# First batch's attention denominators from key sums of their own, an earlier load of the first weights, and a later preparation of the second batch, in a cosformer attention + mixture-of-experts kernel

## Chip, cores, metric

One core of a Trainium2 chip. The metric is the device time of one execution in microseconds (us), lower is better. A clock is the share of TensorE's full speed that was granted, 1.00 or, as half clock, 0.50. The profile's span is one execution's, and is some 1.7 us shorter than the time measured for the same run.

## The reference, cut to what matters

```python
def phi(x, c, s):                        # q, k, v: (8 batches, 8 heads, 576, 64)
    r = np.maximum(x, 0.0)
    return np.concatenate([r * c, r * s], axis=-1)
q_p = phi(q, cos_w, sin_w)
k_p = phi(k, cos_w, sin_w)
kv = np.einsum('bhsf,bhsd->bhfd', k_p, v)
z = np.sum(k_p, axis=2)
num = np.einsum('bhsf,bhfd->bhsd', q_p, kv)
den = np.einsum('bhsf,bhf->bhs', q_p, z)[..., None] + 1e-06
x = num / den                            # then as (4608, 512)
# gates exp(x @ w_gate), 8 rounds of row and column balancing; then for 8 experts
#   out += P[:, e] * (relu(x @ w1[e]) @ w2[e])
```

## The kernel before

The first 60 us prepare the attention of the eight batches one after the other and begin the first expert's two layers as soon as a batch is there. The work is written in "slots": after each piece of the first expert (first-layer tile `ft4` to `ft7`, then halves of second-layer tiles) the functions hung on that slot are issued. Program order is kept on each engine (in the trace before, VectorE's `q_p` at 34.35 us stood behind a `zsel` that had waited 2.84 us), so the slot decides who stands behind whom. A "turn" transposes a third of one head pair's q on TensorE, and an "eviction" copies a result out of TensorE's output memory.

```python
te, ve, se = ...            # TensorE, VectorE, ScalarE, each kept in written order

def prep_k(b, hk):          # relu of k: ScalarE for b >= 1, VectorE for b == 0
def prep_kp(b, hk):         # k_p = relu(k) * (cos | sin), VectorE
def prep_v(b, hk, copy):    # copies v beside a column of ones, into v_aug
def prep_q(b, hk):          # q_p = q * (cos | sin), VectorE; three q_p buffers;
                            #   for b >= 2 a DMA transposes it into q_pT, on SyncE's queue
def turn(b, hk, i):         # b < 2: three matmuls with the identity turn a third of q_p,
                            #   ScalarE or VectorE evicts it with a relu
def sums_begun(b, half):    # k_p^T [v | 1]: numerator matrix, and z from the column of ones
def sums_made(b, half, ps): # kv_sb (ScalarE) and zsel = z spread over a mask (VectorE)
def denominators(b):        # 24 matmuls zsel x q_pT, then epsilon, reciprocal,
                            #   and hi, hl: the reciprocal made ready for TensorE in f16
def attend(b, hk):          # needs hl and kv_sb: divides, writes xT

# first batch
for hk in range(HK):
    prep_q(0, hk)
    for i in range(3):
        turn(0, hk, i, True)
for hk in range(HK):
    prep_k(0, hk)
    prep_kp(0, hk)
keep_busy(16)               # idle 128x128 matmuls
for half in range(2):
    prep_v(0, 2 * half, se.copy)
    prep_v(0, 2 * half + 1, (se.copy, ve.tensor_copy)[half])
    begun.append(sums_begun(0, half))
    keep_busy((4, 6)[half])
... sums_made(0, 0..1), epsilons(0), denominators(0), keep_busy(34)
for hk in range(HK):
    attend(0, hk)
    prep_k(1, hk)           # the second batch's k, under the first batch's attention
    prep_kp(1, hk)
    if hk >= 2:
        prep_v(1, hk - 2, se.copy)
    ...                     # ft0 to ft3 as xT fills
prep_v(1, 2, se.copy)
prep_v(1, 3, ve.tensor_copy)
# second batch, by slot: prep_q(1, 0) and sums at 4; sums and prep_q(1, 1) at 5;
# turns of head pair hk at 5 + hk, with prep_q(1, hk + 2); denominators at 8; attend at 11 to 14
# third batch: k, q, v from slot 11 on; transposes by DMA.  Fourth batch's loads follow.
```

The softmax here doesn't subtract the row's maximum and nothing guards it: scores larger than these inputs give would overflow.

## Time and profile before

| | kernel before |
|---|---|
| time, median of its runs | 986.6 us (985.36 to 986.98) |
| TensorE busy | 969.9 of 984.8 us, mean clock 0.997 |
| first batch's attention starts | 23.16 us (its first weight load, from which the prediction counts, 23.11) |
| `ft4` starts | 30.55 us |
| second batch's attention starts | 43.69 us |
| third batch's denominators start | 57.25 us |

A window is a stretch of 3.41 us at clock 0.50, of which this trace has two (15.70 to 22.52 us). The landmarks come from the timeline of TensorE: the start in us, the length, then what ran. A batch's attention starts with its first matmul on `hl,acc_hi`, its denominators are the matmuls on `zsel`.

```profile
43.69 0.41 PE L109 MATMUL small_ps<-hl,acc_hi 96*128 96x192 f16 x3
...
57.25 0.75 PE L109 MATMUL small_ps<-q_pT,zsel 128*32 128x192 f16 x18
58.52 0.35 PE L109 MATMUL small_ps<-q_pT,zsel 128*32 128x192 f16 x6 [0.52 <-DMA q_pT<-q_p]
```

The bracket is idle time of the engine just before, and what ended it: the last six waited 0.52 us for a transposed q.

### The profile page before, as it was taken

To read this page: it belongs to the slowest core of one execution; us is meant where nothing else is said; L and a number is where in the kernel's file an instruction comes from. 1 tells how busy PE (TensorE), PEld (TensorE's weight loads), DVE (VectorE), ACT (ScalarE), POOL (GpSimd) and SP (SyncE) were. 2 spreads that over 40 slices of the span, in tenths; PEclk is the share of its full clock that TensorE was granted. 3 is DMA by queue.
4 is the path that set the end of the run, shared out by engine and by line. 5 is a ranking of instruction groups with operands and counts; after the bars stand their busy time and mean duration, and the time that the engine had idled before them with its cause. 6 is when DMAs were issued, how large, how long until landed. Compare 5 with 4: busy or idle time off the path is not lost.

```text
span 984.8 us, 20226 instructions
## 1 busy us (share of the span) xinstructions
PE 969.9 (98%) x7844; PEld 678.4 (69%) x7844; DVE 805.8 (82%) x1830; ACT 568.6 (58%) x1269; POOL 60.6 (6%) x82
## 2 busy tenths in 40 slices
PE   8999999989999999999999999999999999999997
PEld 7545444447777777777777777777777777777775
DVE  5786774789889888988789888988888888988887
ACT  5776665467776555555555555555555555555551
POOL 6311110010000000000000000000000000000001
PEclk8999999999999999999999999999999999999999
DMA  9989990741013410133103400233103401104435
GB/s 162 206 122 162 157 151 9 136 77 47 34 41 68 85 32 25 49 68 68 49 25 69 91 25 25 56 62 67 49 25 68 92 25 27 47 26 117 128 87 129
DMA packets 80336, 73.54 MB, mean 75 GB/s; under 512 B 33264, under 2 KB 72176, under 8 KB 80240
## 3 DMA queue, kind: packets, MB, share of 16 engines
q0 software_dynamic: 27232, 30.94, 20.0%
q1 hardware_dynamic: 52768, 41.06, 17.2%
q8 instruction: 61, 1.00, 0.4%
q14 instruction: 35, 0.29, 0.1%
q10 hardware_dynamic: 240, 0.26, 0.1%
HBM read 83.12 MB, written 12.98 MB: 98 GB/s over the span
## 4 chain that ended last, share of the span: by engine, by line
PE 94%; DVE 2%; DMA 2%; ACT 1%; POOL 1%; issue 0%; POOLq 0%; ACTq 0%; SPq 0%
PE rows_ps L109 34%; PE h_ps L109 28%; PE copied_ps L109 11%; PE p_ps L109 11%; PE y_ps L109 6%; PE small_ps L109 4%; DMA v_ld<-in_v_dram 1%; DMA q_pT<-q_p 0%; DVE acc_hi L847 0%; POOL hs_last L862 0%; DVE P_tok L109 0%; DMA out_dram<-acc_lo 0%; DVE colp L109 0%; ACT u L109 0%; POOL k_ld L201 0%
## 5 line engine op out<-in xcount | busy, mean ns | idle before, releaser
L847 DVE SCALAR_TENSOR_TENSOR acc_lo<-rows_ps,P_tok,acc_lo 128x512 f32<-128x512 f32 (+1 forms) x322 | 203.1, 639 | 74.8 <-PE rows_ps L109 74.7
L109 PEld LDWEIGHTS <-H 128*128 128x128 f16 x2080 | 203.0, 98 | 83.1 <-issue 1.2
L783 ACT CAST u<-h_ps 128x384 f16<-128x384 f32 x288 | 137.6, 478 | 130.7 <-PE h_ps L109 130.7
L109 PEld LDWEIGHTS <-w1e 128*128 128x128 f16 x1632 | 156.4, 98 | 66.2 <-issue 6.0
L777 DVE CUSTOM_DVE_ANT_0 H<-p_ps,u 128x384 f16<-128x384 f32 x329 | 180.9, 550 | 6.7 <-PE p_ps L109 6.6
L109 PEld LDWEIGHTS <-hs 128*128 128x128 f16 x1500 | 146.6, 98 | 56.2
L109 PE MATMUL h_ps<-S,w1e 128*128 128x384 f16 x672 | 164.1, 326 | 1.1 <-ACT u L109 0.9
L109 PE MATMUL p_ps<-xT,T 128*128 128x384 f16 x672 | 164.1, 326 | 0.1
L109 PE MATMUL rows_ps<-V,H 128*128 128x256 f16 x1000 | 150.0, 273 | 0.7 <-DVE acc_hi L847 0.7
L109 PE MATMUL h_ps<-xT,w1e 128*128 128x384 f16 (+1 forms) x616 | 150.1, 350 | 0.2 <-DVE xT L109 0.2
L109 PE MATMUL rows_ps<-w2e,hs 128*128 128x256 f16 x1000 | 150.0, 273 | 0.0
L815 ACT ACTIVATE H<-h_ps 128x384 f16<-128x384 f32 x144 | 70.6, 490 | 95.1 <-PE h_ps L109 95.1
L109 PEld LDWEIGHTS <-T 128*128 128x128 f16 x1008 | 98.1, 98 | 29.5 <-issue 3.1
L109 PE MATMUL rows_ps<-w2e,H 128*128 128x256 f16 (+1 forms) x568 | 91.2, 285 | 0.0
L796 ACT COPY copied_ps<-h_ps 128x384 f32<-128x384 f32 x144 | 67.5, 469 | 36.0 <-PE h_ps L109 35.2
L806 ACT ACTIVATE H<-copied_ps 128x384 f16<-128x384 f32 x144 | 70.8, 492 | 20.4 <-PE copied_ps L109 20.4
L109 PE MATMUL h_ps<-S,T 128*128 128x384 f16 x336 | 81.8, 325 | 0.4 <-ACT copied_ps L109 0.3
L109 PE MATMUL copied_ps<-xT,w1e 128*128 128x384 f16 x336 | 82.1, 326 | 0.0
L109 PE MATMUL copied_ps<-w2e,H 128*128 128x256 f16 x504 | 75.5, 272 | 0.0
L109 PE MATMUL rows_ps<-V,hs 128*128 128x256 f16 x500 | 74.9, 272 | 0.0
L847 DVE SCALAR_TENSOR_TENSOR acc_lo<-copied_ps,P_tok,acc_lo 128x256 f32<-128x256 f32 x126 | 60.0, 476 | 0.4
L847 DVE SCALAR_TENSOR_TENSOR acc_hi<-rows_ps,P_tok,acc_hi 128x512 f32<-128x512 f32 (+1 forms) x56 | 41.3, 737 | 20.6 <-PE rows_ps L109 19.7
(140 smaller groups left out, 956.9 us busy)
## 6 DMA issues: line engine op xcount, KB each, us to landing
S<-x_saved SPq DMA_DIRECT2D x108, 192.0 KB, 2.4
out_dram<-acc_lo SPq DMA_DIRECT2D x62, 128.0 KB, 2.4
w1e<-in_moe_w_dram POOLq DMA_DIRECT2D x7, 1024.0 KB, 9.0
w2e<-in_moe_w_dram POOLq DMA_DIRECT2D x7, 1024.0 KB, 9.6
q_ld<-in_q_dram POOLq DMA_DIRECT2D x16, 288.0 KB, 7.4
k_ld<-in_k_dram POOLq DMA_DIRECT2D x16, 288.0 KB, 8.3
v_ld<-in_v_dram POOLq DMA_DIRECT2D x16, 288.0 KB, 9.4
x_saved<-S SPq DMA_DIRECT2D x18, 192.0 KB, 1.9
```

The lines of the kernel that those rows point to most:

```text
L109: i = getattr(self.engine, name)(*args, **kwargs)
L777: latest = ve._custom_dve(TENSOR_ADD_SAT, out=out, in0=ps[:, 0:TU], in1=t[:], s0=FP32_MAX, s1=0.0)
L783: se.copy(out=t[:], in_=ps[:, 0:TU])
L796: se.copy(out=Y[:, 0:TU], in_=X[:, 0:TU])
L806: se.activation(out=h11, in_=Y[:, 0:TU], func=AF.Relu)
L815: se.activation(out=h12, in_=X[:, 0:TU], func=AF.Relu)
L847: ve.scalar_tensor_tensor(out=a, in0=rows, scalar=P_tok[:, g, self.e : self.e + 1], in1=a, op0=ALU.mult, op1=ALU.add,)
```

## The change

The first attention waited for v. The change takes the denominators' z from k and the cos/sin columns alone (`key_sums`: 72 matmuls of two columns), so that the reciprocal chain can run before v is there; the first batch's v then needs no column of ones and no copy. The start is reordered around that with fewer idle matmuls, all four parts of the first w1 load ahead of the second batch's k and v, and the second and third batches' preparation moves to later slots. The core of the diff:

```diff
-        load_w1(w0, 0, 4, (0, 1))
+        load_w1(w0, 0, 4)
         load(1, 0, "kv")
         load(1, 1, "kv")
-        load_w1(w0, 0, 4, (2, 3))
...
+        cs_half: cos columns, split by head half        # 1 memset, 2 copies, VectorE
...
-            if b:                                       # prep_k: relu on ScalarE
+            if b >= 2:
...
+        def key_sums(half):
+            for i in range(2):
+                for c in range(C):
+                    for a in range(2):
+                        te.matmul(out=z_ps[a * D : (a + 1) * D, 2 * i : 2 * i + 2],
+                                  lhsT=loaded["k", 0, 2 * half + i][:, c],
+                                  rhs=cs_half[:, c, a, :], ...)
+        def key_sums_made(half, z_ps):                  # one zsel instruction per half
...
-        (first batch as shown above)
+        for half in range(2):
+            for hk in (2 * half, 2 * half + 1):
+                prep_k(0, hk)
+            z_ps = key_sums(half)
+            keep_busy(5); epsilons and k_p 0, 1 (half 0), or k_p 2 (half 1)
+            key_sums_made(half, z_ps)
+            if half == 0:
+                denominators(0, range(0, 4))
+                keep_busy(10)
+        prep_kp(0, 3)
+        denominators(0, range(4, 8))
+        for half in range(2):
+            sums_made(0, half, sums_begun(0, half))
+            keep_busy((3, 16)[half])
         for hk in range(HK):
             attend(0, hk)
-            prep_k(1, hk)
-            prep_kp(1, hk)
-            if hk >= 2:
-                prep_v(1, hk - 2, se.copy)
-        prep_v(1, 2, se.copy)
-        prep_v(1, 3, ve.tensor_copy)
+        keys((0, 1))                    # prep_k, prep_kp, prep_v of the second batch
...
-                (second batch's slots as shown above)
+                at(0, 5, lambda: begun.append(sums_begun(1, 0)))
+                at(0, 5, keys, (2, 3))
+                at(0, 6, lambda: sums_made(1, 0, begun[0]))
+                at(0, 7, lambda: begun.append(sums_begun(1, 1)))
                 for hk in range(HK):
+                    at(0, 7, prep_q, 1, hk)
                     for i in range(3):
+                        at(0, 7, turn, 1, hk, i)
                     if hk == 0:
+                        at(0, 7, lambda: sums_made(1, 1, begun[1]))
+                at(0, 9, denominators, 1)
...
-                    (11, prep_k, 0), (11, prep_q, 0), (12, prep_k, 1), (12, prep_kp, 0), ...
+                    (12, prep_q, 0), (12, prep_k, 0), (13, prep_q, 1), (13, prep_k, 1),
+                    (14, prep_kp, 0), (14, prep_v, 0, se.copy), (15, prep_kp, 1),
+                    (15, prep_v, 1, se.copy), (15, prep_k, 2), (15, prep_k, 3),
```

## The prediction

> **What bounds the kernel now.** I read the page first: busy tenths, then the chain that ended last.

> ```profile
> PE   8999999989999999999999999999999999999997
> PE 94%; DVE 2%; DMA 2%; ACT 1%; POOL 1%; issue 0%; POOLq 0%; ACTq 0%; SPq 0%
> ```

> TensorE is the bound: 969.9 of 984.8 us busy, 94% of the chain. The change touches only the first two batches' preparation and a few slots for the third, all before 60 us. In the table by stretches TensorE is busy 10.00 of every 10 us from 60 to 190 us, and later code is unchanged. So **the whole effect is how much earlier or later TensorE reaches the third batch's denominators (58.5 us)**. TensorE idles under 15 us in all, so 2% (19.7 us) is out of reach.

> Then the chain in order of time for the start, and the stretches cut at the edges of the low clock:

> ```profile
> 5.31 8.55 DMA v_ld<-in_v_dram
> 13.88 1.25 ACT acc_lo L109 x2
> ...
> 16.10 1.16 PE small_ps L109 x36
> 17.26 0.75 PE y_ps L109 x6
> 18.01 2.19 PE small_ps L109 x28
> 20.20 3.12 PE y_ps L109 x34
> ```

> ```profile
> 12.29:15.70 3.41, 1.16 (x43) 0.91 (x41) 2.38 (x5) 2.02 (x5) 1.54 (x3) 1.00 1.34 199
> 15.70:19.11 3.41, 3.41 (x61) 2.32 (x62) 0.73 (x5) 1.15 (x5) 2.08 (x3) 0.50 1.27 205
> 19.11:22.52 3.41, 3.41 (x44) 3.09 (x39) 2.08 (x3) 0.00 (x0) 1.43 (x2) 0.50 1.23 204
> 8.00:11.41 3.41, 2.94 (x33) 1.99 (x31) 2.68 (x5) 3.38 (x10) 2.41 (x4) 1.00 1.16 185
> ```

> The chain waits for v (landed 13.86), copies it, makes k'v sums, denominators, and 34 idle matmuls (y_ps x34)[...]. Columns of the second fence after the stretch are PE, PEld, DVE, ACT, POOL busy, clock, DMA share, GB/s.[...]

> **What the change leaves waiting** shows in the timeline of the second batch:

> ```profile
> 31.82 0.69 ACT L109 COPY acc_lo<-v_ld 128x576 f16<-128x576 f16 x1
> ...
> 33.75 0.43 ACT L109 CAST kv_sb<-small_ps 128x128 f16<-128x128 f32 x2
> ...
> 34.04 0.39 DVE L109 TENSOR_TENSOR zsel<-acc_hi,small_ps 128x64 f16<-128x64 f16 x2 [2.84 <-ACT kv_sb L109]
> 34.35 0.75 DVE L109 TENSOR_TENSOR q_p<-q_ld,acc_hi 128x1152 f16<-128x1152 f16 x1
> 35.02 0.55 DVE L109 TENSOR_SCALAR q_pT<-small_ps 128x384 f16<-128x384 f32 x1
> ```

> VectorE's zsel waits behind ScalarE's kv_sb, which stands behind v copies and relus. VectorE then alternates q_p and evictions of turned q until 40.38; TensorE fills that with ft6, ft7 and four second-layer matmuls. The second batch's first attention matmul is at 43.69, the common point I compare at.

> [...]two stretches of 3.41 us at 0.50, after one 34% busy; one that is 86% busy by the records kept 1.00.[...] 16 gate matmuls of 8 columns took 0.38 us in the chain, 24 ns each.[...] The zsel above held the already loadable q_p for 2.84 us[...]. So the compiled order, which I compared between the kernels, decides.

> **The change part by part.**

> (a) *First denominators without v.* Added: 2 x 36 two-column matmuls (36 x 24 ns = 0.9 us each, an estimate from the gates). Removed: the v copies (3 ACT, 1 DVE). The added cosine copies make VectorE wait for the second sine (done 4.29), so its set-up ends near 6.6 instead of 5.0 and the first q_p near 7.4; TensorE is in its 80 idle matmuls until 7.6, so this is hidden. Then: turns of q end near 11.5; key sums to 12.5, 5 idle matmuls and the epsilons to 13.2; zsel 12.85; half the denominators (24 took 0.77 us at full clock, so 0.4) to 13.65; ten idle matmuls to 14.2. The second k lands 13.03, two relus 0.6 -> 13.66; key sums 14.2 to 15.1; zsel 15.5; denominators to 16.0; k_p to 16.2; reciprocal 1.35, hi 0.31, hl 0.41 -> **18.3**, against 22.39 before. TensorE meanwhile does both k'v sums (0.74 each) and 16 + 3 idle matmuls (56 ns) to 18.5. So attention starts near **18.5 instead of 23.11: 4.6 us gained**, if the clock stays full.

> (b) *Attention of the first batch.* The second batch's k leaves it. Then TensorE limits it: 4 x 0.85 + 16 x 0.22 plus one start-up wait = 7.1 us against 7.4. ft4 starts at 18.5 + 7.1 = 25.6, before 30.5: **4.9 ahead**.

> (c) *w1 first.* Landings are 1.3 to 1.5 us apart at about 205 GB/s. Before, w1 parts 3 and 4 landed at 25.6 and 26.9; moved ahead they land near 19.7 and 21.0, so ft4 does not wait. k and v of the second batch come 2.7 us later (k 22.4 and 25.2, v 23.8 and 26.7); w2 is still complete near 34.6.

> (d) *Second batch.* ScalarE in compiled order from 25.1: four relus (2.06) to 27.2; two v copies (1.3) to 28.5; two relus (1.1); two v copies (1.3) to 30.9; relu ft6 0.6; kv_sb at 31.5. TensorE waits near 1.2 us for the v copies before its sums. zsel ends near 32.0 to 32.4 (34.43 before): the lead is **down to 2.2**. Now q_p of head pair 0 comes after zsel (before: done at 30.46 to 31.2), and each further q_p comes after the evictions of the pair before, all in slot 7. From zsel: q_p 0.67, turns and kv_sb and second zsel 2.4 (as in the trace) -> 35.1; then three q_p (2.0), five VectorE evictions (2.5) and four hand-overs (1.3) -> 41.0, TensorE's last turn near 40.1. Unlike before, nothing fills TensorE from 31.5 to 40.1 but 36 turns (36 x 56 ns = 2.0 us). Then 8 second-layer matmuls 1.75, denominators 0.7 -> 42.6; den, reciprocal, hi, hl 2.55 -> attention at **45.2, against 43.69: 1.5 lost**.

> (e) *Third batch.* Two k_p now stand ahead of the last two q_p, so the last transposed q can come 0.67 us later; before, TensorE already waited 0.5 us there. Since 2.2 us of the chain there is transfer during other loads, I count 0 to 0.7, middle 0.4.

> Sum: 986.4 + 1.5 + 0.4 = 988.3 at full clock.

> **Rivals.**
> 1. *The clock drops in the turn phase.* 2.0 us of matmul in 8.6 is 23%, under the 34% that halved it before; 3.4 us or more of dense matmul would then run at half speed, costing 1.7 (one window) to 3.4 us (two): 990 to 992. Against it: in 8 to 11.4 us, 33 turns of 56 ns, 54% by streaming, kept full clock, so I do not know where the limit is. The key sums could halve it earlier too[...]: attention would start near 20.5. Half likely.
> 2. *Hand-overs are shorter than I count, and part of the 4.9 us lead stays.* For it: the idle matmul counts (16 ends at 18.5, hl at 18.3) look fitted to a running kernel, and so do the moved slots; one who did that saw the second batch too. Without the losses of (d) it would be 981.5; half of them gives 984 to 985. Against it: the compiled order puts zsel ahead of q_p[...].
> 3. *Transfers set the end of this phase.* If w2 (34.6) were the limit, the gain of (a) would be hidden and the time stay at 986.4. Against it: both kernels start the second layer after it has landed.

> **Range and chances.** Weights: full clock as worked out, 988.3, 0.3; clock lowered, 991, 0.3; part of the lead kept, 984.5, 0.4. The mean is 987.6; I take 987.8, as the order is compiled fact. The range, 983.5 to 992.0, holds rival 2 at its middle and rival 1 up to two half-speed windows. Faster by over 2% would need more than all idle time: 0.01. Slower by over 2% is five times the worst sum: 0.02. Within 2%: 0.97.

> **What would show each step.** (a) hl near 18.3 and attention at 18.5, clock 1.00 from 12 to 20 us. (b) ft4 near 25.6. (c) no wait for w1. (d) a wait of about 1.2 us before the second batch's first sums, on a v copy; turns spread from 33 to 40 with TensorE mostly idle; second attention near 45.2. (e) a wait for the transposed q of 0.5 to 1.2 us. Rival 1: clock 0.50 in stretches after 36 us. Attention before 43.7 would say that (d) is wrong, and the kernel then comes out faster; hl after 20 would say that (a) is. A changed pace after 65 us would break the premise that the rest only shifts.

## The result, and the profile after

Ratios here are the mean time of one kernel's fast runs over that of the other's fast runs of the same rounds, so they are not quite the ratio of the medians quoted. The changed kernel took 993.62 us (median of 4, 990.0 to 994.33) against 986.6: ratio 1.0066, 95% interval 1.004 to 1.0092. It is slower by some 7 us, within 2%, and outside the predicted range.

| from the profiled runs | before | after | predicted after |
|---|---|---|---|
| mean TensorE clock | 0.997 | 0.991 | 1.00 from 12 to 20 us |
| first attention | 23.16 | 22.44 | 18.5 |
| `ft4` | 30.55 | 29.91 | 25.6 |
| second attention | 43.69 | 50.99 | 45.2 |
| third denominators | 57.25 | 64.90 | 58.75 (57.25 + 1.5) |

From the third denominators on, the two kernels run alike: those ended at 58.79 before (where the gate matmuls follow) and at 65.73 after, 6.9 us apart, and TensorE's last matmuls start at 980.19 and 986.86, 6.7 us apart. So the loss lies before 66 us, as the prediction assumed of any effect. (The profiled run after was also 1.2 us slower from its last matmul to its end, 5.16 us against 3.98; experiment 9, the same kernel again, was not, with 3.98.)

The landmarks after, in TensorE's timeline, with the waits in the second batch's turns:

```profile
22.44 0.68 PE L109 MATMUL small_ps<-hl,acc_hi 96*128 96x192 f16 x3
...
36.36 0.51 PE L109 MATMUL small_ps<-ident,q_p 128*128 128x128 f16 x6 [0.80 <-DVE q_p L109]
...
39.44 0.68 PE L109 MATMUL small_ps<-ident,q_p 128*128 128x128 f16 x9 [1.83 <-DVE q_p L109]
41.56 1.14 PE L109 MATMUL small_ps<-ident,q_p 128*128 128x128 f16 x9 [1.45 <-DVE q_p L109]
43.70 1.14 PE L109 MATMUL small_ps<-ident,q_p 128*128 128x128 f16 x9 [1.00 <-DVE q_p L109]
44.64 3.00 PE L109 MATMUL y_ps<-w2e,hT 128*128 128x512 f16 x8
...
50.99 0.42 PE L109 MATMUL small_ps<-hl,acc_hi 96*128 96x192 f16 x3 [0.35 <-DVE hl L109]
...
64.90 0.90 PE L109 MATMUL small_ps<-q_pT,zsel 128*32 128x192 f16 x24
```

Nine turns take 0.68 us at 39.44 and 1.14 us at 43.70: the same instructions at two clocks. Eight second-layer matmuls take 3.00 us; before they took 1.89. VectorE beside it, with the same four `q_p` that TensorE waits for:

```profile
20.09 0.41 DVE L109 SCALAR_TENSOR_TENSOR hl<-hi,lo,den 96x192 f16<-96x192 f16 x1
...
35.25 0.39 DVE L109 TENSOR_TENSOR zsel<-acc_hi,small_ps 128x64 f16<-128x64 f16 x2 [2.38 <-ACT kv_sb L109]
35.55 0.75 DVE L109 TENSOR_TENSOR q_p<-q_ld,acc_hi 128x1152 f16<-128x1152 f16 x1
...
38.64 0.75 DVE L109 TENSOR_TENSOR q_p<-q_ld,acc_hi 128x1152 f16<-128x1152 f16 x1
...
40.76 0.75 DVE L109 TENSOR_TENSOR q_p<-q_ld,acc_hi 128x1152 f16<-128x1152 f16 x1
...
42.90 0.75 DVE L109 TENSOR_TENSOR q_p<-q_ld,acc_hi 128x1152 f16<-128x1152 f16 x1
```

`hl`, which lets the first attention begin, is done at 20.5 us (22.39 before), and `zsel` stands in front of the first `q_p`, as the compiled order said. The clock is the one thing not in the order. Here are the stretches of 3.41 us cut at its edges; the columns are PE, PEld, DVE, ACT and POOL busy us with their instructions, the granted clock, DMA share, GB/s.

```profile
9.33:12.74 3.41, 2.71 (x61) 2.07 (x59) 3.35 (x7) 3.41 (x10) 1.75 (x3) 1.00 1.19 199
12.74:16.15 3.41, 3.41 (x49) 2.12 (x47) 1.39 (x4) 0.21 (x1) 1.83 (x3) 0.50 1.37 196
16.15:19.57 3.42, 3.42 (x82) 2.73 (x80) 2.23 (x3) 0.21 (x2) 1.71 (x3) 0.50 1.42 199
19.57:22.98 3.41, 3.41 (x57) 2.97 (x55) 0.86 (x3) 0.65 (x4) 1.86 (x3) 0.50 1.21 206
33.22:36.63 3.41, 2.61 (x49) 1.47 (x48) 1.06 (x3) 2.66 (x7) 2.04 (x3) 1.00 1.21 207
36.63:40.04 3.41, 1.17 (x17) 0.78 (x14) 1.83 (x5) 1.36 (x5) 1.17 (x3) 1.00 1.21 206
40.04:43.46 3.42, 1.22 (x11) 0.88 (x9) 2.50 (x5) 1.42 (x3) 0.36 (x1) 0.50 1.21 206
43.46:46.87 3.41, 3.17 (x15) 1.80 (x16) 1.30 (x3) 0.49 (x1) 0.72 (x1) 0.50 1.21 206
```

Two losses are to be seen. At the start, three stretches run at half clock (before: two, somewhat later), and the sixteen idle matmuls that were to end as `hl` does hold the first attention until 1.9 us after it. In the turns a stretch in which TensorE is busy 1.17 of 3.41 us is followed by two at half clock. In both, 3.41 us is the step. The table cannot say what each costs in time, or what the new order would have done without them. That was the first thing to test.

### The profile page after: what moved, and what is told of

Its sections match the earlier page's. It is cut to its first block, busy times and chain, and to the rows that moved or that the text cites. A ratio compares the mean times of both kernels' runs of the same rounds, so it can differ in the third digit from the quotient of the medians.

```text
span 992.6 us, 20327 instructions
## 1 busy us (share of the span) xinstructions
PE 973.6 (98%) x7895; PEld 680.1 (69%) x7895; DVE 806.8 (81%) x1833; ACT 565.2 (57%) x1263; POOL 60.7 (6%) x82
## 4 chain that ended last, share of the span: by engine, by line
PE 94%; DVE 2%; ACT 2%; POOL 0%; issue 0%; DMA 0%; ACTq 0%; SPq 0%; POOLq 0%
PE rows_ps L109 34%; PE h_ps L109 28%; PE copied_ps L109 11%; PE p_ps L109 11%; PE y_ps L109 7%; PE small_ps L109 4%; ACT q_pT L109 0%; ACT hT L109 0%; ACT acc_lo L109 0%; DVE q_p L109 0%; DVE acc_hi L891 0%; POOL hs_last L906 0%; DVE P_tok L109 0%; DMA out_dram<-acc_lo 0%; DVE colp L109 0%
## 5 line engine op out<-in xcount | busy, mean ns | idle before, releaser
L109 PEld LDWEIGHTS <-H 128*128 128x128 f16 x2080 | 203.0, 98 | 83.1 <-issue 1.2
L109 PEld LDWEIGHTS <-w1e 128*128 128x128 f16 x1632 | 156.6, 98 | 67.2 <-issue 6.7
L109 PEld LDWEIGHTS <-hs 128*128 128x128 f16 x1500 | 146.6, 98 | 56.2
L109 PE MATMUL h_ps<-S,w1e 128*128 128x384 f16 x672 | 164.1, 326 | 1.1 <-ACT u L109 0.9
L109 PE MATMUL p_ps<-xT,T 128*128 128x384 f16 x672 | 164.1, 326 | 0.1
L109 PE MATMUL rows_ps<-V,H 128*128 128x256 f16 x1000 | 150.0, 273 | 0.7 <-DVE acc_hi L891 0.7
L109 PE MATMUL h_ps<-xT,w1e 128*128 128x384 f16 (+1 forms) x616 | 149.9, 350 | 0.6 <-ACT hT L109 0.5
L109 PE MATMUL rows_ps<-w2e,hs 128*128 128x256 f16 x1000 | 150.0, 273 | 0.0
L109 PEld LDWEIGHTS <-T 128*128 128x128 f16 x1008 | 98.1, 98 | 29.3 <-issue 2.8
L109 PE MATMUL rows_ps<-w2e,H 128*128 128x256 f16 (+1 forms) x568 | 91.2, 285 | 0.0
L850 ACT ACTIVATE H<-copied_ps 128x384 f16<-128x384 f32 x144 | 70.8, 492 | 20.4 <-PE copied_ps L109 20.4
L109 PE MATMUL copied_ps<-xT,w1e 128*128 128x384 f16 x336 | 82.1, 326 | 0.0
L109 PE MATMUL h_ps<-S,T 128*128 128x384 f16 x336 | 81.8, 325 | 0.3 <-ACT copied_ps L109 0.3
L109 PE MATMUL copied_ps<-w2e,H 128*128 128x256 f16 x504 | 75.5, 272 | 0.0
L109 PE MATMUL rows_ps<-V,hs 128*128 128x256 f16 x500 | 75.0, 272 | 0.0
L891 DVE SCALAR_TENSOR_TENSOR acc_hi<-rows_ps,P_tok,acc_hi 128x512 f32<-128x512 f32 (+1 forms) x56 | 41.3, 737 | 20.5 <-PE rows_ps L109 19.7
```

What stands on the lines that cost most here:

```text
L109: i = getattr(self.engine, name)(*args, **kwargs)
L850: se.activation(out=h11, in_=Y[:, 0:TU], func=AF.Relu)
L891: ve.scalar_tensor_tensor(out=a, in0=rows, scalar=P_tok[:, g, self.e : self.e + 1], in1=a, op0=ALU.mult, op1=ALU.add,)
```

## The experiments

Twelve experiments ran, each beside the kernel before; all were correct. Theory: the new order loses about 1.7 us, as predicted, and the two half-clock stretches lose the rest. Rivals: the order itself loses the 7 us through waits I had not counted (then a full clock changes little); or the transfers do, since w1 now goes ahead.

**1. Fill the turn phase.** Idle matmuls ahead of each head pair's turns keep TensorE busy where it only waited; nothing else changes.

```diff
                 for hk in range(HK):
                     at(0, 7, prep_q, 1, hk)
+                    at(0, 7, fill, (12, 28, 22, 22)[hk])    # 128x128 idle matmuls
                     for i in range(3):
```

> The changed kernel with idle matmuls put into the turn phase of the second batch (12, 28, 22 and 22 ahead of the turns of the four head pairs), nothing else. Theory C (the half clock of 40.0 to 46.8 us costs time of its own): clock 1.00 through the turn phase, the last two groups of nine turns take 0.67 us again instead of 1.14, the eight second-layer matmuls after them 1.8 us instead of 3.0; about 2 us less than the changed kernel, near 991.5. Theory O (only the order of q_p behind zsel and the evictions counts, the clock is a bystander): within 0.5 us of the changed kernel's 993.6.

989.37 us (median of 6; before 986.65), ratio 1.0031. The runs fall in two groups: 987.65, 987.89 and 987.98 at mean clocks 0.999 to 1.000, and 990.76, 991.15 and 991.85 at 0.994 to 0.997. The expected 991.5 is met by the slower group alone. The profiled run is of the fast group, with full clock until its matmuls end. Its stretches and its timeline:

```profile
12.74:16.15 3.41, 3.40 (x100) 2.42 (x98) 2.36 (x7) 0.12 (x1) 1.79 (x3) 1.00 1.37 196
...
36.63:40.04 3.41, 3.19 (x51) 2.73 (x49) 2.37 (x5) 1.23 (x3) 1.49 (x3) 1.00 1.21 206
40.04:43.46 3.42, 3.42 (x49) 1.86 (x48) 1.57 (x4) 0.28 (x2) 0.72 (x1) 1.00 1.21 206
```

```profile
18.37 0.41 PE L109 MATMUL small_ps<-hl,acc_hi 96*128 96x192 f16 x3
...
25.64 1.89 PE L109 MATMUL h_ps<-xT,w1e 128*128 128x512 f16 x8
...
44.89 0.42 PE L109 MATMUL small_ps<-hl,acc_hi 96*128 96x192 f16 x3 [0.35 <-DVE hl L109]
```

This run is the prediction at full clock: 18.37 for 18.5, 25.64 for 25.6, 44.89 for 45.2, and about 987.8 us for 988.3. Filling the turns takes away the half clock there. That the start's drop comes in some runs and not in others, with an unchanged program, would make the two groups, 3.4 us apart (mean 987.84 and 991.25); only the fast group has a trace, so for the slow group this is read from the mean clock and not shown.

**2. Put the second and third batches' order back.** The key sums, the start and the early w1 stay.

```diff
-            if b >= 2:                       # and the old lines in attend's loop, slots 4 to 9
+            if b:                            # and the third batch's list, as before
```

> The changed kernel with the second and third batches' preparation put back as in the kernel before (k relu on ScalarE, k_p inside the first attention, turns spread over four slots with first- and second-layer matmuls between them, third batch's list); own key sums and the earlier w1 loads stay. Theory O/C (the loss is made in the second batch's new order, by waits and half clock): the whole loss of 7 us goes, 985.5 to 987, second attention at 43 to 44 us. Rival (the loss comes from w1 ahead of k and v, or from the key sums): still 990 or more.

986.90 us, ratio 1.0007 (0.9995 to 1.0019): the 7 us are gone, but nothing is won. The first attention is at 19.69 and the second at 40.65, 3.0 us ahead of before; the third denominators are at 57.81, behind before's 57.25. Where the lead went, in VectorE's and TensorE's timelines and the chain of waits of this kernel:

```profile
53.23 0.76 DVE L109 TENSOR_TENSOR q_p<-q_ld,acc_hi 128x1152 f16<-128x1152 f16 x1 [2.75 <-DMA q_pT<-q_p]
```

```profile
54.72 0.46 PE L109 MATMUL small_ps<-acc_lo,k_p 64*128 64x65 f16 x18 [2.61 <-DVE k_p L109]
```

```profile
43.79 9.35 DMA q_pT<-q_p
```

The fourth `q_p` of the third batch needs one of three buffers; the first is free only when its transpose has landed, 9.35 us after it was issued. Until about 50.5 us the queues move some 205 GB/s of the fourth batch's loads, issued earlier. VectorE waits with `k_p` behind it, and TensorE waits for that `k_p`. The wait has a second cost: the stretch around it, 52.57 to 55.98, has TensorE busy for 1.26 of 3.41 us, and the next one, to 59.39, runs at half clock, where the eight first-layer matmuls take 2.78 us in place of 1.89.

**3. Only the third batch's list put back.**

```diff
-                    (12, prep_q, 0), (12, prep_k, 0), (13, prep_q, 1), ...
+                    (11, prep_k, 0), (11, prep_q, 0), (12, prep_k, 1), ...
```

> The changed kernel with only the list of the third batch's preparation put back. In the changed kernel two k relus on ScalarE stand ahead of the first relu of the second token block, and TensorE waits about 0.9 us there (59.9 to 60.4 and 61.4). Theory: 0.3 to 0.9 us less than the changed kernel, near 993. Rival (that order hides the transposed q, whose wait of 0.5 us is gone): no gain, or 0.5 us more.

992.98 us, ratio 1.0059 (1.0047 to 1.0071) against 1.0066 and 1.0058 for the changed kernel. In the trace a 0.48 us wait of TensorE for ScalarE (two k relus stood ahead of a first-layer relu) is gone and this stretch takes 6.84 us in place of 7.57, but in time the difference is not to be told from scatter.

**4. Fill the start with narrow matmuls.** Three idle matmuls after each turn, and the key sums with 64 columns in place of two.

```diff
                 turn(0, hk, i, True)
+                keep_busy(3)
...
-                            rhs=cs_half[:, c, a, :],
+                            rhs=cs_half[:, c, a, :].unsqueeze(2).to_broadcast([P, 2, 32]),
```

> The changed kernel with three more idle matmuls after each group of three turns of the first batch, and key sums with 64 moving columns instead of 2 (same results, columns repeated). Theory C (the first half-clock stretch, 12.9 to 23.0 us, takes away the gain of the key sums): clock 1.00 to 23 us, hl near 18.5 and attention at 18.5 to 19.5 instead of 22.4, about 3.5 us less in all, near 990. Rival (the start is not what limits the second batch: its v lands 26.7): attention early, time within 1 us of 993.6. If the clock still drops, matmuls of this density do not hold it and nothing is told.

993.61 us, ratio 1.0076: no gain. The clock at the start is now kept, and `hl` is done at 18.85, but at 18.4 us TensorE stops without anything to wait for, and half clock follows from 20.5 (0.53 in 20.4 to 24 us; the drop in the turns comes as in the changed kernel):

```profile
20.46 1.76 PE L109 MATMUL y_ps<-ones_sq 128*128 128x128 f16 x15 [2.04 <-issue]
```

The remedy failed for a reason of its own: 2.04 us put down to issue. With some 36 more narrow matmuls in the same time, and the transfers at about 200 GB/s, a supply of instructions that comes too late was my guess, and experiment 8 uses few, wide matmuls for that reason. The traces agree with it. DMA queue 8, of kind "instruction", brought 61 packets of 16 KB in the profile before, and TensorE had 15,688 matmuls and weight loads: some 257 to a packet, an estimate which takes all of them to be TensorE's. In experiments 4, 8, 11 and 12 the idle time put down to issue comes after 350 matmuls (in 4) or 222 (in the other three): 128 apart, which with their weight loads is 256. In the profiled run after, packets had landed at 13.02 and 20.68, and the matmuls after those counts started at 16.9 and 25.9, without idle time. That a packet came late in the four is still a guess, and no run changes the supply itself.

**5 and 6. Hold the fourth batch's q and v back until after the third batch's `q_p`,** in experiment 2's kernel, and as a control in the kernel before.

```diff
-                        at(1, 0, load, b + 2, half)
+                        at(1, 0, load, b + 2, half, "k")
...
+                        at(1, 1, load, b + 1, half, "qv", True)   # waits for VectorE's last
                     at(j, 1, sums, b, 0)
```

> The run with the old second and third order (own key sums, w1 first), and besides the fourth batch's q and v loads held until the third batch's q_p are made; its k loads stay. In the run without this hold the second attention was 3.0 us ahead of the kernel before (40.65 against 43.69), and the lead was lost in a wait of 2.6 us: the transpose of the third batch's first q took 9.4 us from issue to landing, until the loads of the fourth batch had drained near 50.5. Theory T (transfers queued ahead of the transposes give the lead back): with 1.15 MB (some 5.6 us at 205 GB/s) out of the way the first transposes land in 3 to 5 us, the 2.6 us wait goes, the time is 2 to 3 us less, 984 to 985. Rival (held loads then come late for the fourth batch, near 60 us, and make a wait of their own): no gain, with a wait for q_ld or v_ld in 58 to 66 us.

> The kernel before with only the same hold of the fourth batch's q and v. Control for the run above: theory T says that the kernel before has next to no such wait (0.5 us for the last transpose), so 0 to 0.6 us less, 986.0 to 986.7. If it gains 2 us or more, the hold helps by itself and says nothing on the lead.

Experiment 5: 985.62 us, ratio 0.9991 (0.9978 to 1.0004), where 984 to 985 was expected. From second attention to third denominators it takes 13.6 us, where experiment 2 took 17.2:

```profile
43.08 0.41 PE L109 MATMUL small_ps<-hl,acc_hi 96*128 96x192 f16 x3
...
56.64 0.86 PE L109 MATMUL small_ps<-q_pT,zsel 128*32 128x192 f16 x24
```

This profiled run had the half-clock start, so its first attention was at 22.55 and it had no lead to lose: the kernel before, from about the same second attention, takes 13.6 us too. What shows the cause is the transpose, which lands 3.38 us after its issue in place of 9.35, and experiment 11, which has the hold and a lead (second attention at 41.63): there it also lands in 3.38 us, and the stretch takes 13.6 us, while experiment 7, without the hold and at 41.72, takes 17.1. So the wait of experiment 2 was the fourth batch's loads, and is mended. The control: 987.19 us, ratio 1.0007 (986.0 to 986.7 was expected). In the kernel before the held loads fall on the last transposes instead, and TensorE waits longer than the 0.52 us it had:

```profile
59.55 0.35 PE L109 MATMUL small_ps<-q_pT,zsel 128*32 128x192 f16 x6 [1.77 <-DMA q_pT<-q_p]
```

The hold is worth something only where there is a lead to lose.

**7. w1 first, alone,** in the kernel before.

```diff
-        load_w1(w0, 0, 4, (0, 1))
+        load_w1(w0, 0, 4)
...
-        load_w1(w0, 0, 4, (2, 3))
```

> The kernel before with only the order of loads changed: all four w1 parts ahead of the second batch's k and v. Theory: harmless, k and v land 2.7 us later (k 22.4, 25.3; v 23.8, 26.7) and are wanted at 24.1 to 31.8 us in that kernel; the second half's k relu at 26.9 and v copies after 27.5 still find them; within 0.5 us of 986.6. Rival (the load order is part of the loss): over 1 us more.

986.79 us, ratio 1.0004 (0.9992 to 1.0017). It neither costs nor gains: the second attention comes at 41.72, 2.0 us ahead, and TensorE then waits 1.8 us for `k_p`, as in experiment 2. The lead need not be the loads' doing: the start of this profiled run had one stretch at half clock, that of the kernel before two.

**8. Fill the start with wide matmuls,** on top of experiment 1: idle matmuls of 512 columns, one of them after each three turns, 64-column key sums.

```diff
-                    out=idle_ps[:, 0:P], lhsT=ones_sq[:], rhs=ones_sq[:], ...
+                    out=idle_ps[:, 0 : cols * P], lhsT=ones_sq[:],
+                    rhs=ones_sq[:].unsqueeze(1).to_broadcast([P, cols, P]), ...   # cols = 4
...
             for i in range(3):
                 turn(0, hk, i, True)
+            keep_busy(4)
```

> The changed kernel with fill in the turn phase (as in the first run of this study) and with the idle matmuls of the start made 512 columns wide (a quarter of the instructions), one more of them after each three turns of the first batch, and key sums of 64 columns. The filled run was two-valued: 987.7 to 988.0 where the start kept its clock, 990.8 to 991.9 where it halved. Theory C: with the start always busy, all runs are near 987.7 and the clock record near 1.000. Besides, the run with many narrow idle matmuls at the start showed TensorE idle for 2.0 us at 18.4 with nothing to wait for; if that was its instruction supply, it does not occur here. Rival (the drop at the start does not come from low activity): still two-valued.

990.98 us (990.18 to 991.22), ratio 1.0051; clocks 0.998 to 1.000. The clock now stays full in every run and the two groups are one, which supports that the groups of experiment 1 were the start's clock. The time is not the 987.8 of experiment 1's fast group, though: the filling itself delays the first attention to 20.20 (18.37 there), 0.73 us of it idle time put down to issue. The delay is 1.8 us; another 1.0 us comes after the last matmul of the profiled run (5.02 us to its end, 4.04 in experiment 1). Keeping the clock up cost about as much as the drop.

**9. The changed kernel again,** unaltered.

> The changed kernel unaltered, for more runs with their clock records. Theory C: two values, set by whether the half clock also strikes at the start: most runs near 993.5 with a clock record of 0.991, a few near 990 with 0.994; the difference of 3.5 us is the gain of the key sums lost. Rival (the scatter has another cause): times do not go with the clock record.

992.96 us (990.23 to 993.19), ratio 1.0058: the result repeats. Over both sets, six runs at mean clock 0.991 average 993.5 us and three at 0.994 average 990.4. Which drop those three were spared no trace shows. This trace also splits the loss otherwise than the first one: two stretches at half clock at the start (13.72 to 20.55) and three in the turns (37.62 to 47.85), where the first had three and two, five in both.

**10. Another order for the second batch alone,** in the changed kernel: v copies on VectorE, the first `q_p` ahead of `zsel`, second-layer matmuls between the turns of the head pairs.

```diff
+                at(0, 5, lambda: begun.append(sums_begun(1, 0)))
+                at(0, 5, prep_q, 1, 0)
+                at(0, 5, keys, 2)
+                at(0, 5, lambda: sums_made(1, 0, begun[0]))
+                at(0, 6, keys, 3)
+                at(0, 6, turns_of, 0)          # then q_p 1 at 6, turns 1 and q_p 2 at 7,
+                at(0, 6, prep_q, 1, 1)         # turns 2 and q_p 3 at 8, turns 3 at 9
```

> The changed kernel with only the second batch's order after the first attention altered: q_p of each head pair made ahead of the zsel and evictions it stood behind, turns spread over slots 6 to 9 among first- and second-layer matmuls, v copies on VectorE (idle there). Start, w1 first and the third batch's list stay. Theory O: TensorE is never idle for long from 32 to 45 us, clock 1.00 there, second attention 7 to 8 us earlier than the changed kernel's 50.99, near 43; of this lead a part is lost again to the transposes waiting behind the fourth batch's loads; 985.5 to 988. Rival (order is not the cause): above 990.

986.83 us, ratio 1.0006 (0.9993 to 1.0018). With the start still as in the changed kernel, and at half clock in the profiled run (first attention at 22.43), the second attention comes at

```profile
45.46 0.42 PE L109 MATMUL small_ps<-hl,acc_hi 96*128 96x192 f16 x3 [0.34 <-DVE hl L109]
```

and the clock is full from 23 us on. That is 5.5 us ahead of the changed kernel from the same first attention (23.0 us from first to second, against 28.55), and 2.5 us later than I expected; `q_p` still comes 1.7 us late in sum. The order of the second batch, with the clock that it keeps, is thus where most of the 7 us can be had back, without touching start, w1 or third batch.

**11 and 12. All remedies together:** the old order (11) or the order of experiment 10 (12), the old third list, the held loads, and a lighter wide start: one 512-column idle matmul after each three turns of the first two head pairs only.

```diff
+                if hk < 2:
+                    keep_busy(4)             # wide; start with keep_busy(84); 64-column key sums
```

> All remedies with the old second and third order: own key sums, w1 first, fourth batch's q and v held, idle matmuls of the start 512 columns wide with one more after each three turns of the first two head pairs, key sums of 64 columns. The held run was two- or three-valued, 984.1 with clock 0.999 and 985.6 to 985.8 with 0.995 to 0.998. Theory C plus T: always near 984.0, 2 us under the kernel before. If the start slips by 1 us or more as in the wide run before (20.2 instead of 18.4), nothing is lost as long as attention starts by 19.7, when k of the second batch becomes the limit.

> As the run above but with the second batch's new order of this call in place of the old one. Theory: 983.5 to 985.0; the new order takes k and v out of the first attention, so an early start is used in full; the wait for the second batch's k, v and q (landing 22.4 to 29) is what may keep it from more. Rival: v copies on VectorE delay its chain, and it is 1 to 2 us slower than the run above.

Experiment 11: 984.72 us (983.63 to 985.44), ratio 0.9983 (0.9971 to 0.9996), the fastest of all, 0.17% ahead of before at clock 0.999. Experiment 12: 986.91, ratio 1.0002. By the means of the runs the old order is 1.6 us faster (984.75 and 986.35), but the two profiled runs are alike (985.36 and 985.24), and no run says why. In 11:

```profile
41.63 0.41 PE L109 MATMUL small_ps<-hl,acc_hi 96*128 96x192 f16 x3
...
55.19 1.12 PE L109 MATMUL small_ps<-q_pT,zsel 128*32 128x192 f16 x24
```

The first attention is at 19.28, 3.9 us ahead of before; a wait of 0.86 us for ScalarE, which has the second batch's k to do in that attention, and others leave 2.1 at the second and at the third. In time 1.6 us are left of it.

## Why the prediction was wrong

**The step that failed is the condition of (a), "if the clock stays full", and with it the weight of rival 1.** The text saw the mechanism ("The clock drops in the turn phase", "The key sums could halve it earlier too"), called it "half likely" there, gave it 0.3 in the weights, and counted it once, at 990 to 992. Both drops came. The sizes that the runs show:

- The order at full clock: 987.8 (the fast group of experiment 1), predicted 988.3. Both stand against a kernel before whose own start runs two stretches at half clock; its one run at mean clock 1.000 took 985.36.
- By the groups of runs, the drop in the turns: the changed kernel's slower group less that of experiment 1, 993.5 - 991.25 = 2.2 us; of the faster groups 990.4 - 987.8 = 2.6, with the reserve of the next point. Rival 1 had 1.7 to 3.4.
- By the groups, the drop at the start: 991.25 - 987.84 = 3.4 us in experiment 1, 993.5 - 990.4 = 3.1 in the changed kernel, if its faster runs were those spared the start's drop.

These differences add up to the whole by their making, so their sum is no test. The traces give a test: the start is the same program in the changed kernel and in experiment 1, and the turns differ by the fill alone.

| us later than in experiment 1's profiled run (full clock) | after | experiment 9 |
|---|---|---|
| stretches at half clock, start and turns | 3 and 2 | 2 and 3 |
| `ft4` (25.64 there) | 4.27 | 3.27 |
| second attention (44.89) | 6.10 | 6.20 |
| third denominators (58.81) | 6.09 | 6.19 |

The start's drop thus cost 3.3 to 4.3 us and that of the turns 1.8 to 2.9, some 6.1 together: 987.65 + 6.1 = 993.8, where these runs measured 994.33 and 993.19. The range's upper end, 992.0, held two half-speed stretches in the turns and nothing at the start.

**(a)** `hl` near 18.3 and attention at 18.5: at full clock 18.14 and 18.37, so the order and the sum of the durations were right (the key sums took 0.73 us each, not 0.9); in the profiled run after, 20.5 and 22.44. The prediction had set "hl after 20 would say that (a) is" wrong, and it was after 20. The test did its work, and the clock was the cause.

**(b)** From first attention to `ft4` predicted 7.1 us: 7.27 in experiment 1, 7.47 after. Right.

**(c)** No wait for w1: right; experiment 7 shows that the earlier load does nothing by itself.

**(d)** Right in kind: `zsel` ahead of `q_p`, each further `q_p` behind the evictions, TensorE mostly idle in the turns. From first to second attention predicted 26.7, in experiment 1 26.5; with the clock drop 28.55. The predicted 1.2 us wait for v copies before the first sums did not come (about 0.1 us in experiment 1, and the sums 0.3 us longer); the other terms took its place.

**(e)** No wait for a transposed q came: the 24 denominator matmuls run together at 64.90 (0.22 us in experiment 1). A wait of 0.48 us for ScalarE's relus, gone in experiment 3, was there instead, of the size allowed for.

**Rival 2**, that part of the 4.9 us lead stays, had the largest weight, 0.4, and is false for this order: experiment 1 has the full lead at `ft4` and none at the second attention. The idle-matmul counts fit the kernel at full clock (the attention follows them at 18.37, with no wait for the chain), which I read as a sign that whoever wrote it saw it gain; with the same counts the clock of the start fell to 0.50 in the profiled runs after and of experiments 2, 3, 5, 9 and 10, and kept 1.00 in that of experiment 1.

**Rival 3**, transfers, played no part in the changed kernel, which has no lead to lose. It is real one step further: with the order mended (experiment 2) a transposed q behind the fourth batch's loads, with the half clock that the wait brings, takes the 3 us, and with the loads held (experiment 11) a lead of 2.1 us is kept.

An aside of the prediction does not hold, and nothing rests on it: 19.7 us is 3.5 times the loss to 992.0, not five times. The 34 idle matmuls ahead of the first attention ran at half clock until 22.52 in the kernel before.

What stays open: why the start's narrow matmuls keep the clock in one run and lose it in another (see the last section), what TensorE waited for in the 0.65 to 2.04 us put down to issue in experiments 4, 8, 11 and 12, and which drop the faster runs of the changed kernel were spared.

## What to carry to other kernels

When a change thins out a stretch in which TensorE only waits on short hand-overs, lay the prediction on the clock first: give every full-clock stretch of 3.4 us in which TensorE is busy 1.6 us or less the half-speed stretches after it (one to three in these runs), and look at more than one run, since the same program may keep or lose its clock (mean clocks of 0.994 to 1.000 in experiment 1). A lead won early is kept only if every later hand-over, buffer and transfer has room for it, so look for the next place where the program waits before counting it as time. When idle matmuls are added to hold the clock, count the instructions too: in four kernels here they ran into a wait of 0.65 to 2.04 us put down to issue. Whether the second batch's k is better under the first attention than after it, experiments 11 and 12 do not settle.
